# Attention scores of two tile pairs put in (chunk, query) partitions, their probabilities transposed to (tile, key), v loaded to match

## The chip, the cores and the metric

The kernel runs on one core of one Trainium2 chip. Its time is the device time of one execution in microseconds, as the median of several runs. Three runs of the kernel before took 865.67, 867.43 and 867.85 us, median 867.43.

## The reference

Inputs are q, k and v, each [8, 8, 576, 64] (batch, head, sequence, head dimension), and two weight matrices, `w_in` [512, 2048] and `w_out` [2048, 512], all float32.

```
chunk = 64                                  # 576 = 9 chunks
scores = (q_c @ k_c.T) / sqrt(64)           # inside each chunk of 64 positions alone
attn   = exp(scores - rowmax);  attn = attn / (rowsum + 1e-9)
out    = attn @ v_c                         # [8, 8, 576, 64]
x      = out, heads side by side            # [4608, 512]
h      = x @ w_in;  g = h * sigmoid(1.702 * h)
return g @ w_out                            # [4608, 512]
```

The scores are small: one chunk of one head is a 64x64 matrix, and nothing crosses a chunk. The two large products are the feed-forward part.

## The kernel before, in words

The 4608 tokens are 36 tiles of 128, so each tile holds two chunks, c = 0 and 1, of all eight heads. Four tiles make a block (nine blocks). The feed-forward part runs for each block over 16 slices of 128 hidden columns. In step g, for block g // 16 and slice g % 16, TensorE computes `h_g` (lines 706 to 708, twelve matmuls, in two halves `h0_g` and `h_g`), ScalarE the gate (lines 727 and 728), VectorE a low part (line 733), and TensorE adds the result into four output tiles (`o_g_0` to `o_g_3`, lines 742 to 744, three matmuls each). Numbers are split into a high and a low part, so that three fast matmuls stand for one full product. In the first block the weights are also made: loaded, converted and split, on ScalarE and VectorE (lines 200 to 242).

Attention is worked out ahead of the block that needs it. The first four tiles go one at a time (`plan_first`). The other 32 go in 16 pairs, named by their first tile u (`plan_pair`). For pairs 4 and 6 (`pe` true) TensorE transposes q and k (line 477) and the probabilities (line 548); for the others VectorE does (lines 495 and 561). The steps of a pair: `load_v` brings v in two steps, one for each tile (line 271); `s_pe` computes scores (line 513); `s_max`, `s_exp`, `s_sum`, `s_norm` make the softmax; `e_pe` and `e_act` transpose the probabilities and copy them out; `x_pe` multiplies them by v (line 578), which is the context x; `x_hi` and `x_lo` (lines 593 and 596) copy x out as high and low part.

In `s_pe` and `x_pe` a product is a 64x64 by 64x64 one, 32 of them for each pair, and each is issued as two matmul instructions. Such a product uses one quadrant of the 128x128 array: the row half is set by the partitions of its operands, the column half by the partitions of its output. For pairs 4 and 6 before, a score of head h (of the two in a head pair n) takes row half h and output half h; the scores of a tile t fill one PSUM bank. For the other pairs the output half is the chunk c, and the bank is h. In `x_pe` the row half is c (v and the probabilities have a chunk's keys there) and the output half is h.

`load_rows` issues one DMA for each stretch of a tile that lies in one batch (576 is four and a half tiles, so that some tiles take two DMAs of 64 partitions): `spans` cuts them.

The order of all steps on all engines is fixed when the program is built. `Plan` holds each step with an engine, a cost, a rank, what it needs and which buffers it takes and gives. `emit` plays them through with these costs: a free engine takes the ready step of lowest rank whose buffers are free. A step's result reaches another engine after a handover, 2.9 for a DMA step and 0.12 to 0.25 for the engines. At the start the order is listed by hand (`ORDER`, which ends on TensorE at `tp0_4`, the transposes that start at 43.38 us). The costs set only the order in which instructions stand in each engine's queue. In it each engine runs strictly by program order and waits by semaphore.

For pair u in block 1 the ranks start at 4.0 (pair 4) and 10.0 (pair 6); scores have rank + 0.6, the context rank + 1.5, v's loads rank - 1.5. There is one buffer each for v, the transposed q and k, the probabilities and their transposes. All DMAs of these steps are issued by SyncE (SP).

Of the kernel before, what the change touches and what calls it, by code (L numbers as in the profile page):

```python
# [9 lines left out]
F32 = mybir.dt.float32  # L10
# [4 lines left out]
AF = mybir.ActivationFunctionType  # L15
# [3 lines left out]
PE, ACT, DVE, POOL, DMA = "pe", "act", "dve", "pool", "dma"  # L19
# [113 lines left out]
def tile_chunk_attention_ffn(  # L133
# [9 lines left out]
    nc = tc.nc  # L143
# [4 lines left out]
    P = 128  # L148
    CH = 64
# [108 lines left out]
    def spans(t0, n):  # L258

        o = 0  # L260
        while o < n:
            b, s = divmod(t0 + o, S)
            c = min(n - o, S - s)
            yield b, s, o, c
            o += c

    def load_rows(t, u, srcs):

        for i, src in enumerate(srcs):
            for b, s, o, c in spans(u * P, P):  # L270
                nc.sync.dma_start(  # L271
                    t[o : o + c, i], src[b, :, s : s + c, :].rearrange("h s d -> s h d")
                )

    def x_part(t, u):
        c0 = (u % TB) * P
        return t[u // TB][:, :, c0 : c0 + P].rearrange("p n (c i) -> p n c i", c=2)
# [158 lines left out]
    def plan_pair(u):  # L436
# [29 lines left out]
        def load_v(t):  # L466
            if t == 0:
                st["v"] = const.tile([P, 2, H, D], F32, tag="v", name=f"v_{u}")
            load_rows(st["v"][:, t].unsqueeze(1), u + t, (v,))

        def t_pe(t):
            if t == 0:
# [27 lines left out]
        def s_pe():  # L500
            tr = st["tr"]
            sc = ps_a.tile([P, 2, 2 * NP, CH], F32, tag="att", name=f"s_{u}")
            for t in range(2):
                for n in range(NP):
                    for c in range(2):
                        for h in range(2):
                            r = slice(64 * h, 64 * h + 64)
                            cols = slice(t * P + 64 * c, t * P + 64 * c + 64)
                            if pe:
                                o = sc[r, t, 2 * n + c, :]  # L510
                            else:
                                o = sc[64 * c : 64 * c + 64, h, t * NP + n, :]
                            nc.tensor.matmul(o, tr[r, 0, n, cols], tr[r, 1, n, cols], start=True, stop=True)  # L513

            st["s"] = sc.rearrange("p t g j -> p (t g) j" if pe else "p h g j -> p g h j")

        def s_max():
            sc = st["s"]
# [22 lines left out]
            eng.tensor_tensor(st["e"], st["e"], bc(st["r"]), op=ALU.mult)  # L541

        def e_pe():
            e = st["e"].rearrange("p (t n c) j -> p t n (c j)", t=2, n=NP)
            st["ps"] = ps = ps_a.tile([P, 2, NP, P], F32, tag="att", name=f"eTp_{u}")
            for t in range(2):
                for n in range(NP):
                    nc.tensor.transpose(ps[:, t, n], e[:, t, n], ident)

        def e_act():  # L550
            st["et"] = et = const.tile([P, 2 * NP * 2, CH], F32, tag="et", name=f"eT_{u}")
            nc.scalar.activation(et, st["ps"].rearrange("p t n (h i) -> p (t n h) i", h=2), AF.Copy)

        def e_dve(i):
            if i == 0:
# [8 lines left out]
                )  # L564

        def x_pe():
            et = st["et"].rearrange("p (t n h) i -> p t n h i", t=2, n=NP)
            if pe:
                ps = ps_a.tile([P, 2, 2, NP, CH], F32, tag="att", name=f"x_{u}")
                st["x"] = [ps[:, c] for c in range(2)]  # L570
            else:
                st["x"] = [ps_h.tile([P, 2, NP, CH], F32, tag="hp", name=f"x_{u}_{c}") for c in range(2)]
            for t in range(2):
                for n in range(NP):
                    for h in range(2):
                        for c in range(2):
                            r = slice(64 * c, 64 * c + 64)
                            nc.tensor.matmul(  # L578
                                st["x"][c][64 * h : 64 * h + 64, t, n, :],
                                st["v"][r, t, 2 * n + h, :],  # L580
                                et[r, t, n, h, :],
                                start=True,
                                stop=True,
                            )

        def x_to(t, c):

            t0 = (u % TB) * P
            cols = t[u // TB][:, :, t0 : t0 + 2 * P].rearrange("p n (t c i) -> p c t n i", t=2, c=2)
            return cols[:, c]  # L590
# [51 lines left out]
        last = pairs.get(u - 2)  # L642
        if u <= NPE:
            plan.add(
                PE, 2.4 if pe else 1.4, rank + 0.6, s_pe, need=need, make=ev("s"),
                take=["att", "att", "e"], give=["tr"],
            )
        else:

            both = need + last["x"][1]  # L650
            for i in range(2):
                plan.add(None, 0, -1000, None, need=both + [f"h_{rank}"], make=ev(f"hp{i}"), take=["hp"])
            plan.add(
                PE, 2.4, rank + 0.6, lambda: (s_pe(), last["x"][0]()), need=both + [ev("hp0"), ev("hp1")],
                make=ev("s"), take=["att", "att", "e"], give=["tr", "et", "v"],
            )
# [213 lines left out]
```

## Time and profile before

| | |
|---|---|
| median of three runs | 867.43 us |
| profiled execution | 864.62 us |
| span of its instructions | 862.8 us |
| PE (TensorE) busy | 853.4 us, 99% |
| DVE (VectorE) busy | 390.1 us, 45% |
| ACT (ScalarE) busy | 323.5 us, 37% |
| POOL (GpSimd) busy | 27.4 us, 3% |

The profile is of one execution. PE is the matmul engine and PEld its weight loads; SPq is the queue of SyncE, which issues the DMAs. Times of rows are in us from the start of the span; a row of the timeline gives start, duration, engine, line, operation, what is written and read, and how many like instructions are merged in it. Ends of matmuls are modelled and overlap with the next start, so the length of a stretch on PE is read from its first start to the start of the next line.

### The profile page before, as it was taken

To read this page: it belongs to the slowest core of one execution; us is meant where nothing else is said; L and a number is where in the kernel's file an instruction comes from. 1 tells how busy PE (TensorE), PEld (TensorE's weight loads), DVE (VectorE), ACT (ScalarE), POOL (GpSimd) and SP (SyncE) were. 2 spreads that over 40 slices of the span, in tenths; PEclk is the share of its full clock that TensorE was granted. 3 is DMA by queue.
4 is the path that set the end of the run, shared out by engine and by line. 5 is a ranking of instruction groups with operands and counts; after the bars stand their busy time and mean duration, and the time that the engine had idled before them with its cause. 6 is when DMAs were issued, how large, how long until landed. Compare 5 with 4: busy or idle time off the path is not lost.

```text
span 862.8 us, 14377 instructions
## 1 busy us (share of the span) xinstructions
PE 853.4 (99%) x5996; PEld 707.4 (82%) x5996; DVE 390.1 (45%) x510; ACT 323.5 (37%) x468; POOL 27.4 (3%) x20
## 2 busy tenths in 40 slices
PE   8999999999999999999999999999999999999998
PEld 7888887888888888888888888888888888888886
DVE  5899965434534352516162544345343524121111
ACT  5899742423323242424242424233232414222221
POOL 0000000000000000000000000000000000000000
PEclk9999999999999999999999999999999999999999
DMA  9996253342312123302230232123101110010001
GB/s 255 298 347 169 32 103 82 61 67 49 83 33 42 26 51 71 51 2 49 74 64 13 43 76 53 27 42 81 26 0 26 42 32 1 1 49 2 1 0 49
DMA packets 194593, 55.49 MB, mean 64 GB/s; under 512 B 179680, under 2 KB 187872, under 8 KB 194528
## 3 DMA queue, kind: packets, MB, share of 16 engines
q1 hardware_dynamic: 194528, 54.57, 27.2%
q8 instruction: 47, 0.77, 0.4%
q14 instruction: 18, 0.15, 0.1%
HBM read 45.09 MB, written 9.44 MB: 63 GB/s over the span
## 4 chain that ended last, share of the span: by engine, by line
PE 92%; SPq 4%; ACT 1%; DMA 1%; issue 1%; DVE 0%; ACTq 0%
PE po L742 15%; PE po L744 15%; PE po L743 15%; PE hp L706 14%; PE hp L708 14%; PE hp L707 14%; PE s L513 2%; SPq L459 2%; PE x L578 2%; SPq L271 1%; DMA first_b<-in_v_dram 1%; PE qkTp L477 0%; PE x L376 0%; ACT raw L210 0%; SPq L202 0%
## 5 line engine op out<-in xcount | busy, mean ns | idle before, releaser
L733 DVE TENSOR_TENSOR g_l<-hp,g_h 128x512 fp32r<-128x512 f32 (+1 forms) x146 | 99.8, 684 | 343.2 <-ACT g_h L728 342.3
L742 PE MATMUL po<-w,g_l 128*128 128x512 f32 x576 | 226.8, 394 | 0.6 <-DVE g_l L733 0.4
L744 PE MATMUL po<-w,g_h 128*128 128x512 f32 x576 | 224.3, 389 | 0.0
L743 PE MATMUL po<-w,g_h 128*128 128x512 f32 x576 | 224.3, 389 | 0.0
L706 PE MATMUL hp<-x_l,w 128*128 128x512 f32 x568 | 221.4, 390 | 0.0
L708 PE MATMUL hp<-x_h,w 128*128 128x512 f32 x568 | 221.0, 389 | 0.0
L707 PE MATMUL hp<-x_h,w 128*128 128x512 f32 x568 | 221.0, 389 | 0.0
L727 ACT ACTIVATE hp<-hp 128x512 f32<-128x512 f32 (+1 forms) x146 | 84.4, 578 | 226.8 <-PE hp L708 225.4
L728 ACT ACTIVATE g_h<-hp 128x512 fp32r<-128x512 f32 (+1 forms) x146 | 86.6, 593 | 206.1 <-PE po L744 205.0
L742 PEld LDWEIGHTS po<-w,g_l 128*128 128x128 f32 x576 | 108.1, 188 | 24.5 <-DVE g_l L733 0.6
L744 PEld LDWEIGHTS po<-w,g_h 128*128 128x128 f32 x576 | 108.1, 188 | 22.7
L743 PEld LDWEIGHTS po<-w,g_h 128*128 128x128 f32 x576 | 108.2, 188 | 21.7
L708 PEld LDWEIGHTS hp<-x_h,w 128*128 128x128 f32 x568 | 106.6, 188 | 22.2
L706 PEld LDWEIGHTS hp<-x_l,w 128*128 128x128 f32 x568 | 106.6, 188 | 22.2
L707 PEld LDWEIGHTS hp<-x_h,w 128*128 128x128 f32 x568 | 106.6, 188 | 22.1
L561 DVE STREAM_TRANSPOSE eT<-e 32x512 f32<-32x512 f32 x112 | 78.7, 703 | 28.9 <-POOL e L541 27.1
L495 DVE STREAM_TRANSPOSE qkT<-raw 128x1024 f32<-128x1024 f32 x28 | 34.6, 1238 | 34.4 <-PE s L513 28.7
L541 POOL TENSOR_TENSOR e<-e,r 128x1024 f32<-128x1024 f32 x14 | 26.7, 1906 | 695.7 <-ACT hp L727 695.7
L593 ACT ACTIVATE x_h<-x 128x512 fp32r<-128x512 f32 x32 | 17.4, 594 | 57.2 <-PE x L578 57.2
L534 DVE TENSOR_REDUCE z<-e 128x16 f32<-128x1024 f32 x16 | 19.5, 1219 | 22.4 <-ACT e L530 22.4
L596 DVE TENSOR_TENSOR x_l<-x,x_h 128x512 fp32r<-128x512 f32 x32 | 20.6, 685 | 7.8 <-ACT x_h L593 7.8
L513 PEld LDWEIGHTS s<-qkT 64*64 64x64 f32 x1024 | 18.2, 135 | 5.6 <-issue 5.6
(69 smaller groups left out, 426.0 us busy)
## 6 DMA issues: line engine op xcount, KB each, us to landing
out_dram<-ob SPq DMA_DIRECT2D x36, 256.0 KB, 2.1
raw<-in_moe_w_in_dram SPq DMA_DIRECT2D x16, 512.0 KB, 7.5
raw<-in_moe_w_out_dram SPq DMA_DIRECT2D x16, 512.0 KB, 7.7
v<-in_v_dram SPq DMA_DIRECT2D x28, 256.0 KB, 3.3
raw<-in_q_dram SPq DMA_DIRECT2D x144, 32.0 KB, 2.0
raw<-in_k_dram SPq DMA_DIRECT2D x144, 32.0 KB, 2.0
raw<-in_q_dram SPq DMA_DIRECT2D x48, 24.0 KB, 1.9
raw<-in_k_dram SPq DMA_DIRECT2D x48, 24.0 KB, 1.9
```

The source lines that it names most:

```text
L495: nc.vector.transpose(st["tr"][:, i].rearrange("p n (t j) -> p (n t) j", j=32), st["raw"][:, i].rearrange("p n t j -> p (n t) j"),)
L513: nc.tensor.matmul(o, tr[r, 0, n, cols], tr[r, 1, n, cols], start=True, stop=True)
L561: nc.vector.transpose(st["et"][po : po + 32, :, 32 * a : 32 * a + 32], st["e"][pi : pi + 32, :, 32 * b : 32 * b + 32],)
L706: nc.tensor.matmul(hp, wh, xl, start=cc == 0, stop=False)
L707: nc.tensor.matmul(hp, wh, xh, start=False, stop=False)
L708: nc.tensor.matmul(hp, wl, xh, start=False, stop=cc == NCC - 1)
L727: nc.scalar.activation(hp, hp, AF.Gelu_apprx_sigmoid)
L728: nc.scalar.activation(g_t[g][0][:, c], hp, AF.Copy)
L733: nc.vector.tensor_tensor(gl[:, c], hp, gh[:, c].bitcast(F32), op=ALU.subtract)
L742: nc.tensor.matmul(po, gl[:, c], w[:, 0, :], start=j == 0, stop=False)
L743: nc.tensor.matmul(po, gh[:, c], w[:, 0, :], start=False, stop=False)
L744: nc.tensor.matmul(po, gh[:, c], w[:, 1, :], start=False, stop=j == NF - 1)
```

## The change

For pairs 4 and 6 alone:

- scores are written to partition half c (chunk) in place of h, and the bank is h in place of the tile t; the order of the 32 products stays;
- the probabilities of a group are then (chunk, query) in partitions, and a transpose takes (tile, key) of one head and one chunk: eight transposes as before, with (tile, key) in the partitions of the result;
- v is loaded with (tile, key) in partitions and the chunk as a free dimension: for each tile two DMAs of 64 partitions, one for each chunk. For tile 4 these were two already, for tiles 5, 6 and 7 one;
- `x_pe` takes row half t, output half h, and writes the bank t; the loops stay t, n, h, c from the outside in;
- `x_hi` and `x_lo` write one tile each, in place of one chunk of both tiles;
- the planned cost of `s_pe` goes from 2.4 to 1.4 for these pairs.

```diff
         def load_v(t):
...
-            load_rows(st["v"][:, t].unsqueeze(1), u + t, (v,))
+            if not pe:
+                load_rows(st["v"][:, t].unsqueeze(1), u + t, (v,))
+                return
+            for c in range(2):
+                for b, s, o, n in spans(u * P + t * P + c * CH, CH):
+                    nc.sync.dma_start(
+                        st["v"][t * CH + o : t * CH + o + n, c], v[b, :, s : s + n, :].rearrange("h s d -> s h d")
+                    )
...
-                            if pe:
-                                o = sc[r, t, 2 * n + c, :]
-                            else:
-                                o = sc[64 * c : 64 * c + 64, h, t * NP + n, :]
+                            o = sc[64 * c : 64 * c + 64, h, 2 * n + t if pe else t * NP + n, :]
                             nc.tensor.matmul(o, tr[r, 0, n, cols], tr[r, 1, n, cols], start=True, stop=True)
-
-            st["s"] = sc.rearrange("p t g j -> p (t g) j" if pe else "p h g j -> p g h j")
+            st["s"] = sc.rearrange("p h g j -> p (h g) j" if pe else "p h g j -> p g h j")
...
         def e_pe():
-            e = st["e"].rearrange("p (t n c) j -> p t n (c j)", t=2, n=NP)
-            st["ps"] = ps = ps_a.tile([P, 2, NP, P], F32, tag="att", name=f"eTp_{u}")
-            for t in range(2):
-                for n in range(NP):
-                    nc.tensor.transpose(ps[:, t, n], e[:, t, n], ident)
+            e = st["e"].rearrange("p (g t) j -> p g (t j)", t=2)
+            st["ps"] = ps = ps_a.tile([P, 2 * NP, P], F32, tag="att", name=f"eTp_{u}")
+            for g in range(2 * NP):
+                nc.tensor.transpose(ps[:, g], e[:, g], ident)
...
             if pe:
+                et = st["et"].rearrange("p (h n c) i -> p h n c i", h=2, n=NP)
                 ps = ps_a.tile([P, 2, 2, NP, CH], F32, tag="att", name=f"x_{u}")
-                st["x"] = [ps[:, c] for c in range(2)]
+                st["x"] = [ps[:, t].rearrange("p c n i -> p n c i") for t in range(2)]
...
             for t in range(2):
                 for n in range(NP):
                     for h in range(2):
                         for c in range(2):
...
+                            o = slice(64 * h, 64 * h + 64)
+                            if pe:
+                                r = slice(64 * t, 64 * t + 64)
+                                o, vt, e = ps[o, t, c, n], st["v"][r, c, 2 * n + h, :], et[r, h, n, c]
+                            else:
+                                r = slice(64 * c, 64 * c + 64)
+                                o, vt, e = st["x"][c][o, t, n], st["v"][r, t, 2 * n + h, :], et[r, t, n, h]
+                            nc.tensor.matmul(o, vt, e, start=True, stop=True)
...
         def x_to(t, c):
 
+            if pe:
+                return x_part(t, u + c)
...
-                PE, 2.4 if pe else 1.4, rank + 0.6, s_pe, need=need, make=ev("s"),
+                PE, 1.4, rank + 0.6, s_pe, need=need, make=ev("s"),
```

## Rows read from the trace of the kernel before

**Rows 1.** The page's busy times and two of its 40-slice lines (busy tenths of PE; granted TensorE clock in tenths of full speed).

```profile
span 862.8 us, 14377 instructions
PE 853.4 (99%) x5996; PEld 707.4 (82%) x5996; DVE 390.1 (45%) x510; ACT 323.5 (37%) x468; POOL 27.4 (3%) x20
...
PE   8999999999999999999999999999999999999998
...
PEclk9999999999999999999999999999999999999999
```

**Rows 2.** The chain of work that ended last, shares of the span by engine and by line.

```profile
PE 92%; SPq 4%; ACT 1%; DMA 1%; issue 1%; DVE 0%; ACTq 0%
PE po L742 15%; PE po L744 15%; PE po L743 15%; PE hp L706 14%; PE hp L708 14%; PE hp L707 14%; PE s L513 2%; SPq L459 2%; PE x L578 2%; SPq L271 1%; DMA first_b<-in_v_dram 1%; PE qkTp L477 0%; PE x L376 0%; ACT raw L210 0%; SPq L202 0%
```

**Rows 3.** Busy time of each engine from 43 to 116 us: the stretch, its length, then busy us (and instructions) of PE, PEld, DVE, ACT and POOL, granted clock, DMA share and GB/s.

```profile
43.00:116.00 73.00, 72.63 (x570) 60.19 (x569) 70.82 (x76) 63.02 (x74) 0.00 (x0) 1.00 0.64 176
```

**Rows 4.** Timeline of PE at the scores of pairs 4, 6 and 8, each with the row behind it.

```profile
60.19 2.08 PE L513 MATMUL s<-qkT 64*64 64x64 f32 x64
62.20 0.50 PE L706 MATMUL hp<-x_l,w 128*128 128x512 f32 x1
...
97.74 2.08 PE L513 MATMUL s<-qkT 64*64 64x64 f32 x64
99.75 0.50 PE L742 MATMUL po<-w,g_l 128*128 128x512 f32 x1
...
117.83 1.16 PE L513 MATMUL s<-qkT 64*64 64x64 f32 x64
...
118.92 0.50 PE L742 MATMUL po<-w,g_l 128*128 128x512 f32 x1
```

**Rows 5.** Timeline of PE at the contexts of pairs 4 and 6. The rows from 112.34 to 113.47 are the first and the last of the six matmuls of the first half of h_14.

```profile
80.32 1.16 PE L578 MATMUL x<-eT,v 64*64 64x64 f32 x64
81.41 0.50 PE L706 MATMUL hp<-x_l,w 128*128 128x512 f32 x1
...
112.34 0.39 PE L706 MATMUL hp<-x_l,w 128*128 128x512 f32 x1
...
113.47 0.39 PE L708 MATMUL hp<-x_h,w 128*128 128x512 f32 x1
...
113.79 1.16 PE L578 MATMUL x<-eT,v 64*64 64x64 f32 x64
...
114.88 0.50 PE L706 MATMUL hp<-x_l,w 128*128 128x512 f32 x1
```

**Rows 6.** Timeline of PE, matmuls that had started by 60.20 us (scores of pair 4, first start 60.19) and by 80.34 us (context of pair 4, first start 80.32).

```profile
60.19 0.27 PE L513 MATMUL s<-qkT 64*64 64x64 f32 x2
...
80.32 0.29 PE L578 MATMUL x<-eT,v 64*64 64x64 f32 x4
```

**Rows 7.** A weight load of the feed-forward stream, beside the matmul of 114.88 in the group on the contexts.

```profile
114.99 0.19 PEld L707 LDWEIGHTS hp<-x_h,w 128*128 128x128 f32 x1
```

**Rows 8.** Timeline of SP from 104.5 us: k and q loads of pairs 8 and 10, and the two loads of v for pair 6.

```profile
104.50 3.16 SPq L459 DMA_DIRECT2D raw<-in_k_dram  x4
107.77 0.39 SPq L271 DMA_DIRECT2D v<-in_v_dram  x1
108.25 2.00 SPq L459 DMA_DIRECT2D raw<-in_q_dram  x4
110.30 0.45 SPq L271 DMA_DIRECT2D v<-in_v_dram  x1
```

**Rows 9.** Single loads of v, each with the time from its issue to its landing where that is used: duration of the issue (min/median/max ns), first and last start in us. The load of 110.3 has 128 partitions (pair 6). Those of 433.4 and 434.0 (the two halves of tile 22), 206.7 (second half of tile 13) and 617.7 (second half of tile 31) have 64, as has that of 204.9 (first half of tile 13), issued right behind a load of 128.

```profile
L271 SPq DMA_DIRECT2D v<-in_v_dram x1: 451/451/451, 110.3 to 110.3; - x1
...
DMA to landing us min/median/max: 3.2/3.2/3.2
...
L271 SPq DMA_DIRECT2D v<-in_v_dram x1: 617/617/617, 433.4 to 433.4; - x1
...
DMA to landing us min/median/max: 2.7/2.7/2.7
...
L271 SPq DMA_DIRECT2D v<-in_v_dram x1: 636/636/636, 434.0 to 434.0; - x1
...
DMA to landing us min/median/max: 3.9/3.9/3.9
...
L271 SPq DMA_DIRECT2D v<-in_v_dram x1: 635/635/635, 206.7 to 206.7; - x1
...
DMA to landing us min/median/max: 3.0/3.0/3.0
...
L271 SPq DMA_DIRECT2D v<-in_v_dram x1: 626/626/626, 617.7 to 617.7; - x1
...
DMA to landing us min/median/max: 3.1/3.1/3.1
...
L271 SPq DMA_DIRECT2D v<-in_v_dram x1: 1756/1756/1756, 204.9 to 204.9; - x1
```

**Rows 10.** Timeline of SP at the second load of v for pair 4 and the weight load behind it.

```profile
58.65 0.43 SPq L271 DMA_DIRECT2D v<-in_v_dram  x1
59.13 3.24 SPq L202 DMA_DIRECT2D raw<-in_moe_w_in_dram  x1
```

**Rows 11.** Timeline of DVE: the last of the 16 weight slices (w_15) is made.

```profile
113.17 1.23 DVE L237 TENSOR_TENSOR w<-wtmp,w 128x1024 fp32r<-128x1024 f32 x1 [0.22 <-ACT w L234]
```

**Rows 12.** Timeline of PE: the first matmul of h_15.

```profile
120.42 0.39 PE L706 MATMUL hp<-x_l,w 128*128 128x512 f32 x1
```

More of the change, by code (lines that the diff above doesn't have):

```diff
@@ L543, in e_pe @@
         def e_pe():
-            e = st["e"].rearrange("p (t n c) j -> p t n (c j)", t=2, n=NP)
-            st["ps"] = ps = ps_a.tile([P, 2, NP, P], F32, tag="att", name=f"eTp_{u}")
-            for t in range(2):
-                for n in range(NP):
-                    nc.tensor.transpose(ps[:, t, n], e[:, t, n], ident)
+            e = st["e"].rearrange("p (g t) j -> p g (t j)", t=2)
+            st["ps"] = ps = ps_a.tile([P, 2 * NP, P], F32, tag="att", name=f"eTp_{u}")
+            for g in range(2 * NP):
+                nc.tensor.transpose(ps[:, g], e[:, g], ident)
         def e_act():
             st["et"] = et = const.tile([P, 2 * NP * 2, CH], F32, tag="et", name=f"eT_{u}")
-            nc.scalar.activation(et, st["ps"].rearrange("p t n (h i) -> p (t n h) i", h=2), AF.Copy)
+            nc.scalar.activation(et, st["ps"].rearrange("p g (c i) -> p (g c) i", c=2), AF.Copy)
         def e_dve(i):
@@ L566, in x_pe @@
         def x_pe():
-            et = st["et"].rearrange("p (t n h) i -> p t n h i", t=2, n=NP)
             if pe:
+                et = st["et"].rearrange("p (h n c) i -> p h n c i", h=2, n=NP)
                 ps = ps_a.tile([P, 2, 2, NP, CH], F32, tag="att", name=f"x_{u}")
-                st["x"] = [ps[:, c] for c in range(2)]
+                st["x"] = [ps[:, t].rearrange("p c n i -> p n c i") for t in range(2)]
             else:
+                et = st["et"].rearrange("p (t n h) i -> p t n h i", t=2, n=NP)
                 st["x"] = [ps_h.tile([P, 2, NP, CH], F32, tag="hp", name=f"x_{u}_{c}") for c in range(2)]
@@ L576, in x_pe @@
                         for c in range(2):
[L577 to L584, printed above, removed]
+                            o = slice(64 * h, 64 * h + 64)
[6 more added lines that the diff above has]
+                            nc.tensor.matmul(o, vt, e, start=True, stop=True)
         def x_to(t, c):
+            if pe:
+                return x_part(t, u + c)
             t0 = (u % TB) * P
```

## The prediction

> **What bounds the kernel now.** I read the page's busy times and slices first, then the chain. TensorE is busy 853.4 of 862.8 us at granted clock 1.0 in every slice [rows 1], and the chain that ended last is 92% PE [rows 2]. The program is in order on each engine, so whatever lengthens or shortens a PE stretch, or makes PE stand, appears whole in the end time, unless PE would have waited there anyway. Only two of the 20 attention groups (4 tiles, 16 pairs) are touched, pairs 4 and 6, both inside the first 125 us, so I read their stretch: from 43 to 116 us PE is busy 72.63 of 73.00 us and DVE 70.82, ACT 63.02 [rows 3]. PE has no slack there; DVE has hardly any.
>
> The profiled execution took 864.62 us, span 862.8 and 1.8 around it; the median of the three timed runs is 867.43, 2.8 above it. I make the sum against the profile and add it to the median.
>
> **Scores (`s_pe`), two pairs.** Before, head h uses row half h and writes output half h, so only two of the four 64x64 quadrants of the array work. The 64 matmul instructions (32 products, two passes each) of pair 4 run from 60.19 to 62.20, when the next line starts: 2.01 us; pair 6 from 97.74 to 99.75: 2.01 [rows 4]. After, output half is c and row half is h: the four quadrants in turn, exactly the form that pair 8 already has, which takes 117.83 to 118.92, 1.09 us [rows 4]. Saved: 2 x 0.92 = 1.84 us, all on the path. This term has rows at both ends; I hold it for sure to 0.1 us.
>
> **Context (`x_pe`), two pairs.** Before: four quadrants in turn, 80.32 to 81.41 and 113.79 to 114.88, 1.09 us each [rows 5]. After, the row half is the outermost loop (tile t), and inside it the pattern is two products on quadrant (t,0), two on (t,64). During a half only two quadrants have work. No row shows this order. Lower bound: nothing lost, 1.09 us, if PE looks far enough ahead to start tile 1's products beside tile 0's; less is excluded, since that is the rate with all four quadrants at work. Upper bound: one quadrant at a time. One quadrant's pitch is 2.01/32 = 63 ns in pair 4's scores [rows 4], so 64 x 63 ns = 4.0 us. In between: two quadrants at work throughout, which is what those scores did, 2.01 us. I take 2.01, the nearest row. That PE does overtake blocked passes is shown: within the first 20 ns of pair 4's context four passes start, and only two of its scores [rows 6], though in program order a product's second pass on the same quadrant comes next. Two quadrants of one row half run together there as well, since all four do. Cost: 2 x 0.92 = 1.84 us, between 0 and 2 x 2.9.
>
> So by busy time the change is worth 1.84 - 1.84 = 0.
>
> A rule of the Trainium skill speaks against this order: TensorE: Matmul & The Clock Gate, Part 3 (what overlaps and what doesn't), says that a weight load overlaps matmuls in flight only where their row groups differ. A context half has a single row group, so by it each half would run one pass after the other, the 4.0 us bound. The trace doesn't bear it out as stated: four quadrants start within 20 ns [rows 6], two of them in each row half, and in the 128-row stream a load starts at 114.99 beside the matmul of 114.88 [rows 5, 7].
>
> **The order.** `x_pe` keeps its planned cost, `s_pe` falls from 2.4 to 1.4 in the planner's clock (which sets only the order). In that clock nothing on the DMA queue depends on the scores: the loads of raw 8 stand ahead of pair 6's v by rank, and v's second step comes free at 110.70, worked through from the costs and handovers in the code (first step of v from 102.90: 1.0 and 2.9; second step: 1.0 and 2.9). PE in the planner is without a gap, so each of its boundaries behind both scores moves 2.0 forward. Before, the boundary ahead of the first half of h_14 was 112.72 and that half ran ahead of the context of pair 6; after, it is 110.72, just past 110.70, and the context has the lower rank. It should go ahead of that half. The margin is 0.02, and earlier softmax steps reshuffle DVE and ACT, so I give this order two in three. What PE reaches early, it can also stand at.
>
> **v of pair 6.** Before, two loads of 128 partitions, issued on SP at 107.77 and 110.30 with four q loads between [rows 8]; the second lands 3.2 us later [rows 9], 113.5, and its half of the context starts about 114.3: covered by under 1 us. After, four loads of 64 partitions. Such halves exist where a tile crosses a batch: each took 617 to 636 ns to issue, against 451 [rows 9], and they landed 2.7, 3.9, 3.0 and 3.1 us after issue [rows 9]. With 0.04 between issues: first pair 107.77 and 108.43, q from 109.11, four of them for 2.05 [rows 8], second pair 111.16 and 111.82, landed 111.82 + 3.0 = 114.8. Bounds: halves issued at 0.39 each and 2.7 to landing give 114.0; 3.9 to landing gives 115.7; one half issued behind a full load took 1.76 [rows 9], so later is possible. SP issues without a gap there [rows 8] and waits for no score, so its time doesn't move forward with PE.
>
> When does PE get there? The first half of h_14 starts at 112.34 before [rows 5]. After: 112.34 - 1.84 (both scores) + 0.92 (context of pair 4) = 111.42, plus 0.09 for the change of shape = 111.5. Tile 0's half needs only the first two loads (landed about 111.5) and takes 1.0: 112.5. Tile 1's half waits for 114.8: a stall of 2.3 us (1.5 to 3.2). Behind it on PE stand h_14 and everything after; ACT and DVE wait for x but nothing that PE soon needs.
>
> **Sum:** -1.84 + 1.84 + 2.3 = +2.3 us: 866.9 on the profile, 867.43 + 2.3 = 869.7 as median.
>
> **At nothing.** The softmax, transposes and evictions keep instruction count and size. The added load of pair 4's v (one whole into two halves) is at 58.65, and the weight load behind it sits 3.24 us in issue anyway [rows 10]: SP waits there for transfers, whose bytes don't change. Without that cover v of pair 6 comes 0.6 us later, and so does the stall's end. Weights: the last one is made on DVE from 113.17, ready by 114.4 [rows 11], and is first used at 120.42 [rows 12], so 6 us of slack remain when PE is 2 us early. The earlier exp of pair 4 delays w_8 and w_9 in the planner, by about what PE finds other work for.
>
> **Rivals.**
> (a) The order stays: the context of pair 6 after the half h (or another step of about 1.4) takes most of the wait. PE gets there 1.36 us later by its own work, 112.9, half 113.9, stall 0.9. +0.9, 868.3. For it: the margin of 0.02 and a reshuffled ACT. Against: PE in the planner has no gap, and any gap it might gain still leaves the context first.
> (b) The context keeps the four-quadrant rate. PE reaches it at 110.6, first two loads at 111.5, half 0.55; it stands until 114.8, ends 115.35 instead of 114.88 and without the half h (1.36): +1.8, 869.2. For it: the overtaking of [rows 6]. Against: to fill four quadrants it would have to reach over a whole half, 32 passes.
> (c) Slower: quadrants of one row half take turns, 4.0 us per context. Place: L578 of both pairs; it decides as soon as a context takes over 2.4 us, for then the sum passes 0.3% whether v is late or not. Pair 6's context is reached at 112.34 - 1.84 + 2.92 + 0.09 = 113.5, its first half ends 115.5, v is there, no stall: -1.84 + 5.84 = +4.0, 871.4. For it: alternation AABB is in no row, and the skill's rule names it. Against: [rows 6].
> (d) It does what the busy time could at best: four-quadrant rate and v in time (v landing at 112, or the context planned 3 us later): -1.84, 865.6. Against: SP's issue times.
>
> **Chances.** Forecast 45% (own range +1.2 to +3.4), (a) 22, (b) 12, (c) 13, (d) 8. A measurement can tell 0.3%, 2.6 us, from no change. Slower by that: a third of the forecast (late landing, 115.1 or after), nearly all of (c): 29%. Faster by that: only the far tail of (d): 4%. Within: 67%. The range for 8 in 10: leaving out most of (d) below and the end of (c) above, 866.3 to 871.9.
>
> **What would show it.** Scores of pairs 4 and 6 at 1.1 us from first start to the next line; contexts at 2.0, in two halves of 1.0, only two starts within 20 ns; for pair 6 a gap of about 2 us in the middle of L578, released by a v DMA; its first matmul ahead of the first half of h_14; v's last load issued near 111.8. It is wrong if the context takes 1.1 or over 2.5 us, or if L578 of pair 6 runs without a gap.

## The result, and the profile after

873.16 us median over six runs (870.86 to 874.09), against 866.76 for the kernel before on the same chip (six runs, 865.67 to 867.85): a ratio of 1.0072, 95% interval 1.0059 to 1.0085. The change makes the kernel 0.72% slower, some 6 us. The forecast was 869.7, its range ended at 871.9, and slower by over 0.3% had a chance of 29%.

The profiled execution took 873.28 us, 8.66 more than that of before; 2.1 of these 8.66 are there because the profile of before (864.62) lies that far below its median. The page, for [rows 1]; the slice that holds 109 to 131 us has lost TensorE time and clock:

```profile
span 871.5 us, 14379 instructions
PE 857.7 (98%) x5996; PEld 711.2 (82%) x5996; DVE 390.4 (45%) x510; ACT 323.4 (37%) x468; POOL 27.4 (3%) x20
...
PE   7999979999999999999999999999999999999998
...
PEclk9999979999999999999999999999999999999999
```

Timeline of PE (start, duration, then, in brackets, the idle time before and its releaser) at what the change touches, for [rows 4, 5]:

```profile
60.51 1.16 PE L518 MATMUL s<-qkT 64*64 64x64 f32 x64
61.60 0.50 PE L712 MATMUL hp<-x_l,w 128*128 128x512 f32 x1
...
76.31 2.00 PE L588 MATMUL x<-eT,v 64*64 64x64 f32 x64
78.25 0.50 PE L748 MATMUL po<-w,g_l 128*128 128x512 f32 x1
...
93.25 1.16 PE L518 MATMUL s<-qkT 64*64 64x64 f32 x64
94.34 0.50 PE L712 MATMUL hp<-x_l,w 128*128 128x512 f32 x1
...
114.15 0.30 PE L588 MATMUL x<-eT,v 64*64 64x64 f32 x2 [2.29 <-DMA v<-in_v_dram]
114.91 1.44 PE L588 MATMUL x<-eT,v 64*64 64x64 f32 x30 [0.46 <-DMA v<-in_v_dram]
117.38 0.47 PE L588 MATMUL x<-eT,v 64*64 64x64 f32 x2 [1.04 <-DMA v<-in_v_dram]
118.44 1.97 PE L588 MATMUL x<-eT,v 64*64 64x64 f32 x30 [0.59 <-DMA v<-in_v_dram]
120.34 0.79 PE L712 MATMUL hp<-x_l,w 128*128 128x512 f32 x1
...
125.63 0.49 PE L748 MATMUL po<-w,g_l 128*128 128x512 f32 x1
```

Each score block takes 1.09 us instead of 2.01, the context of pair 4 takes 1.94 instead of 1.09. The context of pair 6 runs ahead of h_14, is reached at 111.7 and is done at 120.34. PE stands four times, each time for a load of v, 2.29 + 0.46 + 1.04 + 0.59 = 4.38 us. Then h_14's twelve matmuls take 5.29 us (120.34 to 125.63), at a pitch of 0.43 us instead of 0.227. Stretches of that time say why (their length, the busy us of PE, PEld, DVE, ACT and POOL, then granted clock, DMA share and GB/s):

```profile
111.70:115.50 3.80, 1.05 (x23) 0.78 (x24) 3.29 (x4) 1.54 (x2) 0.00 (x0) 1.00 0.53 105
115.60:125.80 10.20, 8.58 (x59) 6.92 (x56) 2.44 (x3) 1.08 (x2) 0.00 (x0) 0.50 0.54 102
```

After 3.8 us in which PE was busy for 1.05, the granted clock is 0.50, the 1.2 GHz level, for 10.2 us, although PE works through most of these.

So the profile adds up: PE reached that context 0.64 earlier than the step lay before (the scores gained 1.84, the context of pair 4 gave back 0.85, the rest is the start of the program). The context took 8.64 us, not 1.09: +7.55. h_14 took 5.29, not 2.72: +2.57. Together +9.5. From there the two kernels run alike but for 0.8 us, and the spans differ by 8.7.

Why v was late: the timeline of SP (start, time in issue), for [rows 8, 10]:

```profile
59.67 1.28 SPq L474 DMA_DIRECT2D v<-in_v_dram  x2
61.09 2.61 SPq L202 DMA_DIRECT2D raw<-in_moe_w_in_dram  x1
63.75 2.13 SPq L206 DMA_DIRECT2D raw<-in_moe_w_out_dram  x1
65.93 0.58 SPq L202 DMA_DIRECT2D raw<-in_moe_w_in_dram  x1
66.55 2.58 SPq L206 DMA_DIRECT2D raw<-in_moe_w_out_dram  x1
...
72.13 6.26 SPq L459 DMA_DIRECT2D raw<-in_q_dram  x4
...
111.06 1.30 SPq L474 DMA_DIRECT2D v<-in_v_dram  x2
112.45 2.05 SPq L459 DMA_DIRECT2D raw<-in_q_dram  x4
114.55 1.28 SPq L474 DMA_DIRECT2D v<-in_v_dram  x2
```

The same stretch in the kernel before, behind the two rows of [rows 10]:

```profile
62.42 1.24 SPq L206 DMA_DIRECT2D raw<-in_moe_w_out_dram  x1
63.70 1.02 SPq L202 DMA_DIRECT2D raw<-in_moe_w_in_dram  x1
64.76 1.13 SPq L206 DMA_DIRECT2D raw<-in_moe_w_out_dram  x1
...
68.55 3.95 SPq L459 DMA_DIRECT2D raw<-in_q_dram  x1
```

SP was 1.0 us late at pair 4's second v step (58.65 to 59.67; nothing of that pair's earlier v step is slower, so this much is carried in from before), 1.96 at the weight load behind it, 3.58 at the first load of raw 8 and 3.29 at pair 6's v. Pair 6's loads themselves behave as forecast: 0.60 to 0.64 us in issue, 2.8 to 3.2 us to landing. But they start 3.3 us later.

### The profile page after: what moved, and what is told of

It is laid out like the page before. It is cut to its first block, busy times and chain, and to the rows that moved or that the text cites. A ratio compares the mean times of both kernels' runs of the same rounds, so it can differ in the third digit from the quotient of the medians.

```text
span 871.5 us, 14379 instructions
## 1 busy us (share of the span) xinstructions
PE 857.7 (98%) x5996; PEld 711.2 (82%) x5996; DVE 390.4 (45%) x510; ACT 323.4 (37%) x468; POOL 27.4 (3%) x20
## 4 chain that ended last, share of the span: by engine, by line
PE 90%; SPq 6%; DMA 1%; ACT 1%; issue 1%; DVE 0%; ACTq 0%
PE po L748 15%; PE hp L712 14%; PE po L749 14%; PE po L750 14%; PE hp L713 14%; PE hp L714 14%; SPq L459 4%; PE s L518 2%; PE x L588 2%; SPq L271 1%; DMA first_b<-in_v_dram 1%; DMA v<-in_v_dram 0%; PE x L376 0%; ACT raw L210 0%; SPq L202 0%
## 5 line engine op out<-in xcount | busy, mean ns | idle before, releaser
L588 PE MATMUL x<-eT,v 64*64 64x64 f32 x1024 | 21.8, 223 | 4.4 <-DMA v<-in_v_dram 4.4
```

What stands on the lines that cost most here:

```text
L588: nc.tensor.matmul(o, vt, e, start=True, stop=True)
```

## The experiments

Theory A: pair 6's v is late, PE stands, the clock falls behind it, and that is the whole loss. Theory B: the loss is in the products themselves, their order or the accumulators. Theory C came after the first three kernels: SP's queue has no slack from 60 to 130 us, so longer v loads make everything behind them late. Line numbers shift by a few between kernels; names stay.

**1. Take the wait, or the order, away.** Three kernels. `early_v` plans pair 6's v one rank earlier, among the loads of raw 8:

```diff
-                DMA, 1.0, rank - 1.5, lambda t=t: load_v(t), need=[ev("v0")] if t else [], make=ev(f"v{t}"),
+                DMA, 1.0, rank - (2.5 if u == 6 else 1.5), lambda t=t: load_v(t), need=[ev("v0")] if t else [], make=ev(f"v{t}"),
```

> The changed kernel with one number altered: the two v steps of pair 6 get rank 7.5 in place of 8.5, so that SP issues them among the loads of raw 8, some 25 us earlier. Theory A (v of pair 6 lands late, PE stands for it, and the clock falls in that stretch): the gaps in the context of pair 6 go, the granted clock stays 1.0, and what is left is the scores' gain and the contexts' price, -1.84 + 2 x 0.86 = -0.1 us against the kernel before: ratio 0.999 to 1.001. Theory B (the order of quadrants in the context, or the new order of steps, costs by itself): still 4 to 6 us slower than before, ratio 1.005 to 1.007.

`rot` lets the four quadrants take turns (chunk outermost, tile innermost):

```diff
-            for t in range(2):
+            for a in range(2):
                 for n in range(NP):
                     for h in range(2):
-                        for c in range(2):
+                        for b in range(2):
+                            t, c = (b, a) if pe else (a, b)
```

> The changed kernel with the two loops over tile and chunk exchanged in the context, so that row halves alternate and four quadrants work in turn; v as in the changed kernel. Theory A: both contexts at 1.09 us, but pair 6 then needs all four loads of v before its fourth product, so PE stands as before until the last of them lands and the clock falls as before: 4 to 7 us slower than before, ratio 1.004 to 1.008. Theory B (quadrant order is the cost): the 6 us go, ratio 0.998 to 1.001.

`late_x` holds pair 6's context back until o_12 is through (`need=... + (["o_12_3"] if u == 6 else [])`).

> The changed kernel with one need added to the plan: the context of pair 6 waits for the last matmuls of step 12, so that it stands about 5.4 us later in PE's queue; loads as in the changed kernel. Theory A: PE finds other work while v lands, the gaps shrink from 4.4 us to under 1, the clock stays 1.0 or falls only shortly: ratio 0.999 to 1.002. Theory B: as slow as the changed kernel, ratio 1.005 to 1.008.

Measured: `early_v` 868.20 (ratio to before 1.0022, 1.0007 to 1.0037), `rot` 870.77 (1.0048, 1.0035 to 1.0061), `late_x` 867.97 (1.0013, 1.0000 to 1.0026). In `rot` PE stands at the context of pair 6 for 2.22 and 3.14 us, released by v, and the clock falls again. In the other two the wait is gone or 0.69 us, and with it go some 4.3 and 5.1 us of the 6.2 (by the ratios). Theory A holds for the bulk; B falls, since the order alone brings back 2.1 us, near the 1.7 that two contexts at 1.09 save, and leaves the wait. But `early_v`, where scores and contexts should balance, is still 1.9 us above the kernel before by the ratio (1.4 by the medians), and its twelve runs spread from 866.15 to 871.69. Its profile (871.69 us) shows a new place, and that of `late_x` (870.48 us) a like one: DVE stands 5.65 us for pair 10's k, and PE later 3.44 us for a g_l. DVE in `early_v`, and then PE:

```profile
126.41 1.25 DVE L502 STREAM_TRANSPOSE qkT<-raw 128x1024 f32<-128x1024 f32 x1 [4.54 <-DMA raw<-in_q_dram]
...
134.62 1.25 DVE L502 STREAM_TRANSPOSE qkT<-raw 128x1024 f32<-128x1024 f32 x1 [1.76 <-DMA raw<-in_q_dram]
135.79 0.65 DVE L739 TENSOR_TENSOR g_l<-hp,g_h 128x512 fp32r<-128x512 f32 x1
```

```profile
136.50 0.80 PE L712 MATMUL hp<-x_l,w 128*128 128x512 f32 x1 [3.85 <-DVE g_l L739]
```

DVE, in order, stands at the transpose for pair 10 until its q lands; the g_l queued behind it frees the accumulator that PE's next h needs. In the kernel before the same place had DVE, and then PE, at:

```profile
128.80 1.25 DVE L495 STREAM_TRANSPOSE qkT<-raw 128x1024 f32<-128x1024 f32 x1 [3.28 <-DMA raw<-in_q_dram]
129.97 0.65 DVE L733 TENSOR_TENSOR g_l<-hp,g_h 128x512 fp32r<-128x512 f32 x1
```

```profile
131.30 0.39 PE L706 MATMUL hp<-x_l,w 128*128 128x512 f32 x1
```

In `early_v` PE went on 0.71 us after that g_l began; here it would have been free to at 130.68 and came at 131.30. DVE already stood 3.28 us for pair 10, and PE missed a stall by 0.6 us. A second profile of the same kernel:

> A second look at the same kernel as early_v, for its profile alone: as there; contexts at 1.94 us each and no gap inside them.

(Its label is a misnomer; the kernel is `early_v`.) 865.60 us; pair 10's first q was issued at 110.9 instead of 115.3, the same wait of PE was 1.15 us, and the clock held. So the second place comes and goes with SP's lateness in each execution.

**2. Both edits, the clock, and the split alone.** `early_rot` is `early_v` and `rot` together. `filler` adds twelve feed-forward-sized products to pair 6's context:

```diff
             for t in range(2):
+                if u == 6:
+                    for _ in range((8, 4)[t]):
+                        nc.tensor.matmul(
+                            ps[:, t].rearrange("p c n i -> p (c n i)"), wt[0][:, 0, :128], x_h[0][:, 0, :],
+                            start=True, stop=True,
+                        )
```

`before_split` is the kernel before with pairs 4 and 6 loading v in halves of 64 rows, to the same places as ever (`nc.sync.dma_start(st["v"][c * CH + o : c * CH + o + n, t], ...)` for each chunk c). `before_again` is the kernel before, for a second profile.

> The changed kernel with both edits: pair 6's v planned one rank earlier, and the context products ordered so that the four quadrants take turns. Theory A (all of the loss is PE standing for pair 6's v, the clock that falls behind it, and two contexts at 1.94 us): no wait in L589 of pair 6, both contexts near 1.1 us, and the 1.84 us of the scores left over: 1.5 to 2 us below the kernel before, some 865. Theory C (the eight v loads of 64 rows where there were four or five make SP late for everything behind them, and that has a price at other places): contexts the same, but PE waits 1 to 4 us for DVE's g_l behind pair 10's late q or k loads, the time is at or above the kernel before, 867 to 869.

> The changed kernel with twelve extra 128x512 products in pair 6's context, 8 ahead of its first half and 4 ahead of its second, written into its own PSUM tile and overwritten: they fill some 1.7 and 0.85 us in which PE stands for v, and change nothing else (their results are not used). Theory A with the clock as a cost of its own: the loads land at the same times, so the context ends at most 0.5 us later than without them, but the granted clock stays at 1.0 behind it, h_14's matmuls keep a pitch of 0.22 us instead of 0.43, and the median is 2.5 to 3.5 us below the changed kernel's, 870. Rival: the clock is not what costs, h_14 would have waited for something else in those 10 us: the clock stays up, and the time stays at 872 to 874.

> The kernel before, with the v loads of pairs 4 and 6 cut into halves of 64 rows each, into the same partitions as before; scores and contexts as before. Theory C (the split alone makes SP late by 1 to 3 us by the time it reaches raw 8 and pair 6's v): first q load of raw 8 issued at 70 to 72 instead of 68.5, pair 6's last v landed at 116 to 118, a wait of 2 to 4 us in the context of pair 6 (in halves by its tile t, both needing both loads' chunks), time 869 to 871. Theory D (SP's lateness comes from the different placing in SBUF, each half into the same 64 partitions, or from run to run, and the split costs its own issues alone, 0.2 us a load): raw 8 at 68.5 to 69.5, v of pair 6 landed at about 114.5, a wait under 1 us, 867 to 868.

> The kernel before once more, for a second profile of it: how far SP's issue times wander from one execution to another. If the lateness of SP seen in the changed kernel is run to run, raw 8's first q load here may stand anywhere from 68 to 73 us; if it belongs to the change, within 1 us of 68.5.

`early_rot`: 871.07 (1.0049, 1.0034 to 1.0064), above `early_v` and level with `rot`. No wait for v, contexts at 1.09 us; but PE reaches pair 10's place 1.7 us earlier than before, DVE stands 6.41 us for pair 10's q, and PE 5.97, with the clock at half for 6.83 us from 131.8, inside that wait. Theory A alone said 865; C said 867 to 869 with waits of 1 to 4 us: the place is right, the size too low.

`filler`: 868.60 (1.0036, 1.0020 to 1.0051), 3.1 us below the changed kernel by the two ratios, although PE does 2.7 us more work (twelve products of 0.227). Stretches of its profile, with the granted clock ahead of the last two columns:

```profile
111.00:116.00 5.00, 5.00 (x50) 3.70 (x48) 3.88 (x4) 1.54 (x2) 0.00 (x0) 1.00 0.65 132
116.00:121.00 5.00, 4.76 (x48) 3.95 (x47) 2.35 (x3) 1.59 (x3) 0.00 (x0) 1.00 0.59 109
```

The clock holds where PE is given something to do. Of its twelve runs nine have a mean granted clock of 0.999 or 1.0 and take 867.85 to 870.03; the three at 0.993 to 0.996 take 871.67 to 874.72. In this profile v was also issued 1.8 us earlier than in the changed kernel's. So the runs show that the clock is a cost of its own, but not its size; that comes from the changed kernel's own rows, 2.57 on h_14 and about 1.0 on the second half of the context (118.44 to 120.34 for 30 of 32 matmuls, where half a context takes 0.97).

`before_split`: 869.97 (1.0036, 1.0022 to 1.0050). The split alone, with scores and contexts as before, costs half of the loss, at the place that theory C names. PE:

```profile
114.11 0.77 PE L585 MATMUL x<-eT,v 64*64 64x64 f32 x32
116.73 0.33 PE L585 MATMUL x<-eT,v 64*64 64x64 f32 x2 [1.85 <-DMA v<-in_v_dram]
117.92 1.12 PE L585 MATMUL x<-eT,v 64*64 64x64 f32 x30 [0.86 <-DMA v<-in_v_dram]
```

The clock is at half for 6.83 us from 117.0. Two of the six runs (870.31 and 869.68) have a mean granted clock of 1.0, so there the loss came without a stretch at half clock; they have no profile. Raw 8 was reached at 71.1, the time that C gave, but not all for C's reason: pair 4's second v step was already 1.8 us late. `before_again` took 865.16 and reached raw 8 at 68.8, 0.3 from the first profile. From the issue of that v step to raw 8 SP took 9.9 and 9.6 us in the two profiles of before, 10.6 in the split one (the halves' longer issue, 0.85, accounts for that), and 11.0 to 12.5 in the ten profiles of kernels with the changed layout and these loads on SP. The rest of the lateness is older than the change: pair 4's first v load, the first thing that it touches, is issued at 49.4 and 49.8 before, and anywhere from 49.2 to 53.2 in these ten, although in all these traces every engine has the same instructions in the same order up to there. The medians, not one profile, show that the split costs: all six runs of `before_split` are above the slowest of the seventeen of before (868.56 against 868.18).

**3. Where the halves go, and SP relieved.** `by_chunk` loads one chunk of both tiles in a step (the halves go to different partitions) and runs the context chunk by chunk, with `rot`'s order. Three kernels issue these v loads on POOL's queue, where POOL's own work stops at 1.3 us and starts again at 125 (`nc.gpsimd.dma_start` for `nc.sync.dma_start`): `pool` is the changed kernel, `pool_rot` has `rot`'s order too, `before_pool` is `before_split` on POOL.

> The changed kernel with each step of v's loads taking one chunk of both tiles (the two halves of a step go to different 64 partitions) instead of both chunks of one tile (both halves to the same 64), and the context in the order that fits it: chunk outermost, four quadrants in turn. Theory C1 (halves into the same 64 partitions slow the transfers behind which SP stands): from the first v load of pair 4 to raw 8's first q load 19.8 us, as in the split kernel of before, and not 21.3 to 21.8; pair 6's v lands 1.5 us earlier than in the changed kernel, the context waits 1 to 2.5 us, time 868 to 870. Theory C2 (the placing does not matter, only the number of loads): 21 us or more between these two, time as with the four-quadrant order alone, 870 to 871.

> The changed kernel with the v loads of pairs 4 and 6 issued on POOL's queue, which does nothing until 125 us, instead of SP's, and with the four-quadrant order of the context. Theory C (SP's queue is the bound between 60 and 130 us, and each load on it makes all behind it later): no wait for v in either context, no wait for g_l behind pair 10's q and k, raw 8 reached 1 us earlier than in the kernel before, both scores 0.92 us shorter: 1.8 us below the kernel before, 865. Rival: the DMA engines and not SP's issues are the bound, so the loads make the others as late from POOL: waits of 1 to 4 us at pair 6 or at pair 10, 867 to 870.

> The kernel before with the v loads of pairs 4 and 6 cut into halves of 64 rows and issued on POOL's queue. It shows what the relief of SP alone is worth. Theory C: nothing was waiting for SP in the kernel before on PE's path, so no gain: 866 to 867, and the changed kernel with the same relief is 1.8 us faster than this one. Rival (engines, not issues): as the split kernel on SP, 869 to 870.

> The changed kernel with the v loads of pairs 4 and 6 issued on POOL's queue, the context in its own order (one row half at a time). The forecast's terms without the stall: scores 1.84 us less, contexts 1.7 us more, no wait for v: 0 to 0.3 us from the kernel before, 866.5 to 867. If v still comes late from POOL: a wait in L588 of pair 6 and 868 or more.

`by_chunk`: 870.25 (1.0050, 1.0030 to 1.0071), 20.9 us from pair 4's first v load to raw 8 and 5.3 us of waits for v. That lies between C1 and C2, and inside the 20.1 to 21.9 of the ten profiles; whether the partitions matter stays open.

The POOL kernels were slower than anything before: `pool_rot` 873.66, `before_pool` 875.62 and `pool` 875.83 (1.0086, 1.0110, 1.0111), which no theory said. POOL in `pool`:

```profile
1.31 0.84 POOL L474 DMA_DIRECT2D v<-in_v_dram  x1 [0.37 <-issue]
6.33 0.69 POOL L474 DMA_DIRECT2D v<-in_v_dram  x1 [4.18 <-issue]
12.03 0.69 POOL L474 DMA_DIRECT2D v<-in_v_dram  x1 [5.01 <-issue]
12.81 0.30 POOL masks.py:199 TENSOR_SCALAR_AFFINE_SELECT ident<-ident 128x128 f32<-128x128 f32 x1
```

Pair 4's v has a free buffer from the start, so its loads were put ahead of the identity matrix that POOL builds, 5 to 6 us each, and PE's first matmul went from 1.36 to 13.16. Behind that start PE waits for v nowhere in all three.

**4. Relief without the start.** `pool6_rot` and `act6_rot` move only pair 6's v, to POOL and to ACT (`queue = nc.gpsimd if u == 6 else nc.sync`, or `nc.scalar`), with `rot`'s order. `pool_late_rot` moves all of it to POOL behind a small write of DVE to pair 4's v tile.

> The changed kernel with only pair 6's v on POOL's queue (its buffer comes free near 82 us, so nothing of it can stand ahead of POOL's ident at the start), pair 4's v on SP, four-quadrant order. Theory C (SP's queue, full from 60 to 130 us, is what makes the loads late): SP has four issues of 0.6 us less between raw 8 and raw 10 than the changed kernel, v_6 is issued 20 us before it is needed: no wait in the context of pair 6, pair 10's q and k at or before their times in the kernel before, no clock fall, 1.84 us of scores left: 865. Rival (pair 4's split loads make everything behind them 1 to 3 us late, and that has a price even so): waits for g_l behind pair 10, 867 or more.

> As the one with pair 6's v on POOL, but on ACT's queue: ACT spends some 2.5 us on four issues, in a stretch (90 to 112 us) where it is idle a quarter of the time. Theory C: v in time, pair 10 in time, 865; at most 0.5 us more where ACT's issue stands ahead of a g_h that PE needs. Rival: ACT stands at an issue (the queue is not empty, or v's buffer is not free) and PE waits 1 to 3 us for g_l: 867 or more.

> All v loads of pairs 4 and 6 on POOL's queue, four-quadrant order, and one small write of DVE to pair 4's v tile, for which the first of these loads waits: so ident comes first on POOL. Theory E (the 10.7 to 12.7 us at the start of the three kernels with POOL loads are ident standing behind three v loads on POOL, and nothing else): PE starts at 1.4 us as in the kernel before, and the rest runs as it did there, 2.5 us shorter than before or 1.8: 864 to 865. Rival: POOL's loads slow the first loads on SP themselves: start later by 2 to 4 us, 866 to 868.

`act6_rot`: 874.84 (1.0096, 1.0080 to 1.0112). The rival, and dearer than it said: ACT stands 11.5 us around its first two loads, which it issues only at 112.44 (what held them back is not shown), and PE waits 8.09 us, until 119.12, for the eT queued behind them, with the clock at half for 10.2 us from 114.2. `pool6_rot`: 866.35 (0.9991, 0.9978 to 1.0004), between theory C's 865 and the rival's 867: no wait for v, but 2.73 us for pair 10 and the clock at half for 3.41. `pool_late_rot`: 866.94 (1.0005, 0.9990 to 1.0020). PE starts at 1.37, so theory E holds for the start; but the write came at 55 us, POOL's loads took 6.0 to 7.6 us each beside the weights, and the context of pair 4 waited 3.37 us.

`pool_gate_rot` makes that write at 25.7 us, right behind the last softmax division of tile 3:

```diff
...
             nc.vector.tensor_tensor(st["e"], st["e"], bc(st["r"]), op=ALU.mult)
+            if u == 3:
+                v_first[4] = t = const.tile([P, 2, H, D], F32, tag="v", name="v_4")
+                nc.vector.memset(t[:, :, 0, 0:1], 0.0)
...
```

`before_gate2` is `before_split` with the same write and the same queue: the relief without the new layout. (`before_gate`, the same with v's loads not cut into halves, has no result.)

> As pool_late_rot, but the small write of DVE for which pair 4's first load waits stands 30 us earlier, at about 25 us: four loads of 6 to 7 us each on POOL then end near 55, 20 us before the context needs them. Theory C (SP's queue as the second bound): no wait for v in either context, raw 8 reached at or before 68.8, pair 10's loads at least as early as in the kernel before, no clock fall: the scores' 1.84 us come through in full, 864 to 864.5, if pair 10's q and k are early enough; if they are only as early as before, PE gets there 1.84 us sooner and waits for them up to 1.2 us: 865 to 865.5. Rival (POOL's transfers cost what SP's issues did): 866 or more.

> The kernel before with the v loads of pairs 4 and 6 in halves on POOL's queue behind the same early write: the relief of SP without the change of layout. Theory C: nothing on PE's path in the kernel before waits for SP, so within 0.7 us of the kernel before, 865.5 to 866.8, and 1 to 2.5 us above the changed layout with the same relief (863.8). Rival: the relief itself is what gains (pair 10 or the rows of pair 6 come earlier and PE stands less): 864.5 or less, no difference between the two layouts.

`pool_gate_rot`: 863.83 us (863.28 to 865.88, twelve runs; 0.9973, 0.9962 to 0.9984): 0.27% faster than the kernel before, and a little below the 864 to 864.5 that was expected. `before_gate2`: 865.60 (0.9990, 0.9981 to 0.9999). The new layout, with SP out of its way and the contexts in `rot`'s order, is worth 0.9983 or 1.5 us, near the 1.84 of the scores; the relief itself 0.9. Without `rot`'s order the contexts would give that back, by an estimate from their lengths (1.94 and 1.09, twice): 1.7 us. `pool` and `pool_rot`, which differ in that order alone, are 2.2 us apart, though the profile of `pool` also has 3.4 us at half clock near 31 us and that of `pool_rot` has none. PE at pair 6, and POOL at the first load of each pair, in `pool_gate_rot`:

```profile
111.51 1.16 PE L594 MATMUL x<-eT,v 64*64 64x64 f32 x64
112.60 0.50 PE L718 MATMUL hp<-x_l,w 128*128 128x512 f32 x1
```

```profile
26.11 0.85 POOL L479 DMA_DIRECT2D v<-in_v_dram  x1 [24.80 <-DVE v L359]
...
78.51 0.69 POOL L479 DMA_DIRECT2D v<-in_v_dram  x1 [33.02 <-PE x L594]
```

Both contexts run through in 1.09 us, every v load is issued over 20 us ahead, and the granted clock is 1.0 over the whole span. The DMA engines show the relief too. The two stretches from 56 to 68 us (last columns: clock, DMA share, GB/s; the share adds up the times of packets, so it can pass 1) in the kernel before, the changed one, and this one:

```profile
56.00:62.00 6.00, 6.00 (x85) 5.08 (x85) 5.68 (x7) 5.42 (x7) 0.00 (x0) 1.00 1.14 289
62.00:68.00 6.00, 6.00 (x35) 4.93 (x32) 5.97 (x7) 6.00 (x7) 0.00 (x0) 1.00 1.11 347
```

```profile
56.00:62.00 6.00, 6.00 (x91) 4.89 (x90) 5.69 (x8) 5.32 (x7) 0.00 (x0) 1.00 1.16 257
62.00:68.00 6.00, 6.00 (x28) 4.97 (x27) 5.93 (x6) 5.97 (x6) 0.00 (x0) 1.00 1.14 286
```

```profile
56.00:62.00 6.00, 6.00 (x87) 4.91 (x89) 5.96 (x7) 5.97 (x8) 0.00 (x0) 1.00 1.06 377
62.00:68.00 6.00, 6.00 (x46) 4.93 (x37) 5.94 (x7) 5.97 (x7) 0.00 (x0) 1.00 1.06 376
```

The share is over 1 in each; with v among the weights the engines move less. The changed kernel moves 560 KB less in these 12 us than the kernel before ((289 + 347 - 257 - 286) GB/s x 6 us), and SP, which was 2.1 to 2.6 us in issue at three of the four weight loads from 61 to 69 us, falls behind. That it stands there until the engines take the load is a reading of these times; no run tests it. From pair 4's first v load to raw 8 the rate was 342 and 338 GB/s in the two profiles of before, 333 in `before_split` and 293 to 324 in the ten with the new layout. So the halves alone lower it little, and what lowers it with the new layout is not shown.

## Why the prediction was wrong, and where it was right

**Right.** The scores (1.09 us each, 1.84 saved). The context at the two-quadrant rate: 1.94 measured, 2.01 taken from pair 4's scores, with two passes started within the first 20 ns as the text said. The order: pair 6's context ahead of h_14, reached at 111.7 (111.5 forecast), though the margin in the planner was 0.02 and the forecast gave it two in three. The place and the releaser of the stall. The halves' issue times and landings. Rivals (a), (b) and (c) did not happen; (c)'s rate is excluded by the row of 76.31. The Trainium skill's rule in TensorE: Matmul & The Clock Gate, Part 3, that a weight load overlaps matmuls in flight only on other row groups, is not borne out: within one row half 64 passes took 1.94 us, 30 ns each, where one quadrant at a time has a pitch of 63. (One bound of the sum is off by its own terms: halves issued at 0.39 each and landed after 2.7 give 113.8, not 114.0; nothing hangs on it.)

**The step that failed** is "At nothing": "SP waits there for transfers, whose bytes don't change". The cover was real for one instruction: the weight load behind pair 4's halves shrank from 3.24 us in issue to 2.61. Over the next three it was gone (1.24, 1.02 and 1.13, together 3.39, became 2.13, 0.58 and 2.58, together 5.29): the weights' bytes did not change, but the rate did (292 GB/s from pair 4's second v step to raw 8, where it was 345). The text gave the price of a lost cover as 0.6 us, the issue alone; SP lost 2.6 between pair 4's second v step and raw 8. `before_split` shows that the split by itself brings that lateness in part and half of the loss.

**The stall** was sized 2.3 us (1.5 to 3.2) and measured 4.38. Its end was put at 114.8 from SP's times of before ("SP issues without a gap there [rows 8] and waits for no score, so its time doesn't move forward with PE"): true, and it does not stand still either. With SP 3.3 us late, tile 0's half, which was to have its loads about when PE came, waited 2.75 us as well. A load's start was taken as a constant of the profile where it is the end of a queue that the change lengthens; and it wanders from profile to profile, against a cover of under 1 us that I had read off one: pair 4's first v load by up to 4 us over the ten, behind the same instructions, by 2.4 between the two profiles of `early_v` and by 0.4 between the two of the kernel before.

**The clock** stands in no term. Every price was a duration at granted clock 1.0, the only level in [rows 1, 3], but the forecast itself had PE standing for 2.3 us in a stretch that had run with no wait at that place. In ten profiles of this study PE stood for 2.7 to 8.1 us in all at one such place, and in each the clock was at half for 3.4 to 10.2 us, from somewhere in the wait or right behind it; in the changed kernel that cost about 3.6 us, nearly as much as the wait. A wait of 1.15 us (the second profile of `early_v`) went without. By the wait alone, 4.38 for 2.3, the forecast would have been 871.8, just inside its range.

**Rival (d)**, -1.84 with v in time, was priced without the next wait. In the kernel before pair 10's q kept DVE 3.28 us and missed PE by 0.6 us, so a PE that comes 1.84 earlier stands there unless SP is earlier too. `early_rot` is that rival and took 871.07; `pool_gate_rot`, with SP relieved, shows what it is worth then: 1.5 us for the layout.

**Open:** why the transfers from 56 to 68 us are slower with the new layout's halves on SP beyond their issue time (`by_chunk`, at 322 GB/s, did not settle it), and what makes SP's times differ before the first v load, where the instructions are the same.

## What to carry to other kernels

Before pricing a longer load at nothing, follow its queue to the next place where someone waits for it, and write down the slack there: here 0.8 us at pair 6 and 0.6 at pair 10, on a queue that was full for 70 us. A gain on the busy engine is worth only what the second-latest chain leaves; relieve that first (an idle engine's queue, loads gated so that they neither stand ahead of the start nor arrive late), and the same layout, with `rot`'s order in the contexts, turned from 0.72% slower to 0.27% faster. Where a forecast makes TensorE stand for microseconds in a stretch that ran without a gap, add the half-clock stretch in or behind it, read from any run that shows one.

## What the runs showed of the hardware

- The granted clock fell to 0.50 while PE still worked in between: in the changed kernel at 115.6, with PE busy 1.05 of the last 3.8 us, and stayed there 10.2 us while PE was busy for 8.58. In the profile of `filler`, with products whose results nobody uses in the waits and v 1.8 us earlier, it held.
- Loads of v with 64 rows follow each other on POOL's queue at 5.0 to 5.7 us for the first three at the start of the program, 5.2 to 7.6 beside the weight loads and 3.0 to 4.4 later, where SP needs 0.6 for the same load; POOL's own work behind them waits (the identity matrix until 12.8 us in `pool`).
- Two column halves of one row half run together: the 32 products of a context, two passes each, took 1.94 us in the changed kernel, one row half after the other.
- A load issued from ACT stands in ACT's order: in `act6_rot` PE waited 8.09 us for an eT behind it.
